# Softplus straight from PSUM on ScalarE, beside an attention that keeps Exp

## The chip, the cores and the metric

One core of a Trainium2 chip (trn2) runs the whole program. The metric is device time in microseconds (us) from start to end of one execution. TensorE (PE) multiplies matrices; PEld is its weight load, which overlaps the multiplication. VectorE (DVE) and ScalarE (ACT) do elementwise work, SyncE (SP) issues most transfers. Every engine runs its own list of instructions strictly in order and waits on counters of the others.

## The reference, cut to what matters

```python
# 4 batches, 8 heads, 576 positions, head size 64; window of 64 positions
attn = exp(scores - max); attn = attn / (sum(attn) + 1e-9)     # scores masked to 0 <= i-j < 64
x = attn @ v                                                    # -> 2304 tokens x 512
h = x @ w_in;  g = maximum(h, 0) + log1p(exp(-abs(h)))          # layer 0: 512 -> 2048, softplus
x = g @ w_out                                                   # 2048 -> 512
h = x @ w_in2; g = where(h >= 1, h, where(h <= -1, 0, (h + 1)**2 / 4))   # layer 1
out = g @ w_out2
```

All arrays are float32.

## The kernel before

**Tokens.** The 2304 tokens go in blocks: layer 0 takes 512, 256, 512, 512, 512 of them, called block 0 to block 4 here. Layer 1 takes the same tokens, the block of 256 last. 128 tokens are a double; there are 18 of them, 0 to 17.

**A step of a layer.** A step takes one group of 128 hidden columns (of 16, index f) for one block; in a block of 256 tokens it takes two groups at once, and for the first four groups of block 0 it takes half the block (the half steps). `g1` (L345) makes h in a PSUM bank from twelve products: weights and activations are each split into a high part (`wh`, `xh`) and a low part (`wl`, `xl`), and three of the four pairings are summed. The activation function then makes g, and `g2` (L357 in layer 0, L365 in layer 1) adds its products into four PSUM banks `y`. `g2` runs two steps late (`LAG = 2`), so between the end of a step's `g1` and the start of its `g2` four other groups of products stand on TensorE. h has two banks: the `g1` two steps later needs the last reader of h to be done.

**Softplus before.** ScalarE takes Abs of h (L383), Exp of the negative (L384), adds 1 (block 0: L386; else L388 on VectorE) and takes Ln (L389). VectorE corrects the rounding with L390 and L391 and adds max(h, 0) in L392, the last reader of h. Outside block 0, `parts` splits g into a high part `gh` (ScalarE, L373) and a low part `gl` (VectorE, L374); block 0 multiplies g undivided with undivided weights `wo`. Exp and Ln stand in one table of functions, which is loaded once, at L63.

**Attention.** The attention of a double is made while the block before it is multiplied: block 1's two doubles during block 0, block 2's four during block 1, and so on; block 0's own come first, the last two of them within the half steps. A double has four pieces, one to a step in blocks of 512: scores for half the heads (`sub_scores`, u = 0, which makes all score products, L220), scores for the other half (u = 1), transposes (L273) with masked evacuations (L286), and the products with v (L305) with the copies to `xh` (L312) and `xl` (L315). Inside `sub_scores`, `a1` copies from PSUM (ScalarE, L245 or L247), `d1` finds the maximum (VectorE, L251 to L253), `a2` takes four Exp with row sums (ScalarE, L257), and `d2` divides (VectorE, L261 to L263).

**Weights.** They arrive as packed words (`raw`, three buffers, SyncE, L116) and are decoded by one ScalarE instruction (L123) and three on VectorE (L124 to L126) in block 0. The input weights are split there (L133, L134); the `wo` are split for the later blocks by the end of block 0 and in block 1.

The code is written in program order, and a scheduler of the framework decides how the pieces interleave on each engine.

Of the kernel before, what the change touches and what calls it, by code (L numbers as in the profile page):

```python
# [8 lines left out]
F32 = mybir.dt.float32  # L9
F32R = mybir.dt.float32r  # L10
I32 = mybir.dt.int32
AF = mybir.ActivationFunctionType
ALU = mybir.AluOpType
# [4 lines left out]
P = 128  # L18
# [21 lines left out]
def tile_window_attention_two_ffn(  # L40
# [10 lines left out]
    V, A, T = nc.vector, nc.scalar, nc.tensor  # L51
# [5 lines left out]
    gpool = ctx.enter_context(tc.tile_pool(name="g", bufs=3))  # L57
    tpool = ctx.enter_context(tc.tile_pool(name="tmp", bufs=2))
# [1 line left out]
    psum = ctx.enter_context(tc.tile_pool(name="psum", bufs=1, space=bass.MemoryType.PSUM))  # L60
    dpool = ctx.enter_context(tc.tile_pool(name="dram", bufs=1, space=bass.MemoryType.DRAM))

    A.preload_act_table_set("natural_log_exp_and_others")  # L63


    ident = cpool.tile([P, P], F32, name="ident")
# [27 lines left out]
    def pt(tag):  # L94
        return psum.tile([P, 512], F32, tag=tag, name=tag, bufs={"y": 4, "h": 2, "a": 2}[tag])
# [130 lines left out]
    def sub_scores(dbl, u, bank):  # L226
        if u == 0:
            p2s[dbl] = apool.tile([P, NP, 2, CB], F32, tag="p2", name="p2")
        pr = p2s[dbl][:, 2 * u:2 * u + 2]
        sel = pr.rearrange("p a s j -> p (a s) j")  # L230
        mx = apool.tile([P, NP], F32, tag="mx", name="mx")
        sm = apool.tile([P, NP], F32, tag="sm", name="sm")

        def pe():
            if u == 0:
                scs[dbl] = score_products(dbl, bank)

        def a1():
            sc = scs[dbl][u]
            first = [s for s in range(2) if (2 * dbl + s) % NCB == 0]  # L240
            for s in first:
                V.memset(pr[:, :, s, :], MASKED)
            if first:
                s = 1 - first[0]
                A.copy(pr[:, :, s, :], sc[:, :, s, 0:CB])  # L245
            else:
                A.copy(pr, sc[:, :, :, 0:CB])  # L247

        def d1():
            sc = scs[dbl][u].rearrange("p a s j -> p (a s) j")  # L250
            V.copy_predicated(sel, msel.rearrange("p (o j) -> p o j", o=1).to_broadcast([P, NP, CB]), sc[:, :, CB:])  # L251
            V.tensor_reduce(mx, sel, axis=AX.X, op=ALU.max)
            sub_dve[dbl, u] = V.tensor_scalar_mul(mx, mx, -SCALE).ins  # L253

        def a2():
            for i in range(NP):
                A.activation(sel[:, i, :], sel[:, i, :], AF.Exp, bias=mx[:, i:i + 1], scale=SCALE,  # L257
                             accum_out=sm[:, i:i + 1])

        def d2():  # L260
            V.tensor_scalar_add(sm, sm, EPS)  # L261
            V.reciprocal(sm, sm)
            V.tensor_tensor(sel, sel, sm.rearrange("p (a o) -> p a o", o=1).to_broadcast([P, NP, CB]), op=ALU.mult)  # L263

        return pe, a1, d1, a2, d2

    def sub_transpose(dbl, bank):
        pr = p2s.pop(dbl)
        tp = pt(bank).rearrange("p (a c i) -> p a c i", a=NP, c=2)

        def pe():
            for a in range(NP):
                T.matmul(tp[:, a].rearrange("p c i -> p (c i)"), pr[:, a].rearrange("p c i -> p (c i)"), ident,  # L273
                         start=True, stop=True, is_transpose=True)

        pts[dbl] = [apool.tile([P, NP, 2, CB], F32, tag=f"pt{s}", name=f"pt{s}", bufs=1) for s in range(2)]
        o, n = slice(CB, P), slice(0, CB)

        def evac(s):
            t = pts[dbl][s]  # L280
            r = (n, o)[s]

            for m, dst in ((mown, o), (mprev, n)):
                if dst is n and (2 * dbl + s) % NCB == 0:
                    continue
                V.tensor_tensor(  # L286
                    t[dst].rearrange("p a c i -> p (a c) i"),
                    tp[r].rearrange("p a c i -> p (a c) i"),
                    m[r].rearrange("p (o i) -> p o i", o=1).to_broadcast([CB, 2 * NP, CB]),
                    op=ALU.mult)  # L290

        return pe, (lambda: None), (lambda: evac(0)), (lambda: None), (lambda: evac(1))
# [26 lines left out]
    def attn_subs(block, early=0):  # L319
        t0, n = block  # L320
        xh = xpool.tile([P, KC, 512], F32R, tag="xh", name="xh")
        xl = xpool.tile([P, KC, 512], F32R, tag="xl", name="xl")
        subs = []
        for i in range(n // P):
            dbl = t0 // P + i
            tag = "y" if i < early else "a"
            tag2 = "a" if i % 2 == 0 or i >= early else "h"
            subs += [
                (lambda dbl=dbl, tag=tag: sub_scores(dbl, 0, tag)),
                (lambda dbl=dbl, tag=tag: sub_scores(dbl, 1, tag)),  # L330
                (lambda dbl=dbl, tag=tag2: sub_transpose(dbl, tag)),
                (lambda dbl=dbl, tag=tag2, i=i: sub_pv(dbl, tag, xh, xl, i * P)),
            ]
        return subs, xh, xl
# [35 lines left out]
    def parts(e, n):  # L370
        gh = gpool.tile([P, 512], F32R, tag="gh", name="gh")[:, :n]
        gl = gpool.tile([P, 512], F32R, tag="gl", name="gl")[:, :n]
        A.copy(gh, e)  # L373
        V.tensor_tensor(gl, e, gh.bitcast(F32), op=ALU.subtract)  # L374
        return gh, gl

    def softplus(h, n, split):

        e = tpool.tile([P, 512], F32, tag="e", name="e")[:, :n]
        u = tpool.tile([P, 512], F32, tag="u", name="u", bufs=1)[:, :n]  # L380
        l = tpool.tile([P, 512], F32, tag="l", name="l", bufs=1)[:, :n]
        g = e if split else gpool.tile([P, 512], F32, tag="gl", name="g")[:, :n]
        A.activation(e, h, AF.Abs)  # L383
        A.activation(e, e, AF.Exp, scale=-1.0)  # L384
        if not split:
            A.activation(u, e, AF.Copy, bias=1.0)  # L386
        else:
            V.tensor_scalar_add(u, e, 1.0)  # L388
        A.activation(l, u, AF.Ln)  # L389
        V.scalar_tensor_tensor(e, u, 1.0, e, op0=ALU.subtract, op1=ALU.subtract)  # L390
        V.tensor_tensor(l, l, e, op=ALU.subtract)  # L391
        V.scalar_tensor_tensor(g, h, 0.0, l, op0=ALU.max, op1=ALU.add)  # L392
        return parts(g, n) if split else (g,)

    def quadratic(h, n, split):

# [40 lines left out]

    xs, ys = {}, {}
    subs, *xs[0, 0] = attn_subs(BLOCKS[0][0], HALF // P)
    nq = 4 * HALF // P  # L440
    for j in (0, 1, 4, 5, 2, 3, 6, 7)[:nq]:
# [34 lines left out]
    for layer, i, f, kf, c0, n in steps:  # L476
# [33 lines left out]
        h = pt("h")[:, :kf * n]  # L510
        for j in range(kf):
            g1(layer, f + j, c0, n, *xs[layer, i], h[:, j * n:(j + 1) * n])
        if len(pend) >= LAG:
            emit_g2(pend.pop(0))
        g = (softplus, quadratic)[layer](h, kf * n, (layer, i) != (0, 0))
        pend.append((layer, i, f, kf, c0, n, g))
    while pend:
# [38 lines left out]
```

## Time and profile before

| | |
|---|---|
| time, 3 runs | 908.78 us median, 906.93 to 909.26 |
| the profiled execution's own time | 910.36 us |
| its span, first to last instruction | 908.6 us |
| TensorE busy | 876.2 us (96%) |
| VectorE busy | 621.7 us (68%) |
| ScalarE busy | 425.8 us (47%) |

The profiled execution is 1.6 us above the median of the three runs, and 1.8 us of its time lie outside the span. Busy shares are averages over stages that differ: 0 to 32 us is the first attention, 32 to 75 us the half steps, 75 to 170 us the rest of block 0, 170 to about 230 us block 1, then blocks 2 to 4 up to 519 us, then layer 1.

### The profile page before, as it was taken

How to read it: one execution, taken by the hardware profiler on the slowest of the kernel's cores; microseconds unless marked ns; L12 is line 12 of the kernel's file. 1: busy time of each engine (PE TensorE's matmuls, PEld its weight loads, DVE VectorE, ACT ScalarE, POOL GpSimd, SP SyncE). 2: the span in 40 equal slices, each digit the busy share in tenths (PEclk: the TensorE clock that was granted, in tenths of full speed). 3: DMA queues.
4: the chain of work that ended last, by engine and by line, in shares of the span. 5: the costliest groups of instructions: out<-in, count | busy, mean ns of one | idle time of the engine just before them, and what ended most of it. 6: DMA issues, size and time to landing. Idle time of an engine off the chain costs nothing.

```text
span 908.6 us, 13022 instructions
## 1 busy us (share of the span) xinstructions
PE 876.2 (96%) x4984; PEld 713.6 (79%) x4984; DVE 621.7 (68%) x1166; ACT 425.8 (47%) x958; POOL 1.5 (0%) x10
## 2 busy tenths in 40 slices
PE   3889999899999999999999999999999999999998
PEld 2677656699888888888888888888888888888897
DVE  5899899797777787777999799854335333533342
ACT  5577684555455555554766455432223222322221
POOL 0000000000000000000000000000000000000000
PEclk9999999999999999999999999999999999999999
DMA  8474642334211231200632254120002000200010
GB/s 282 164 217 144 226 155 70 117 82 117 81 41 54 71 116 48 70 1 28 211 110 93 83 195 147 62 93 0 1 1 94 1 0 1 70 1 0 1 48 23
DMA packets 45374, 75.42 MB, mean 83 GB/s; under 512 B 4864, under 2 KB 21760, under 8 KB 45312
## 3 DMA queue, kind: packets, MB, share of 16 engines
q1 hardware_dynamic: 42912, 70.01, 23.9%
q10 hardware_dynamic: 2400, 4.59, 1.4%
q8 instruction: 39, 0.64, 0.3%
q14 instruction: 23, 0.19, 0.1%
HBM read 65.14 MB, written 9.44 MB: 82 GB/s over the span
## 4 chain that ended last, share of the span: by engine, by line
PE 83%; DVE 8%; DMA 3%; ACT 3%; issue 2%; SPq 0%; ACTq 0%; DVEq 0%
PE h L345 40%; PE y L365 22%; PE y L357 17%; DMA raw<-in_w 3%; PE a L305 2%; PE a L220 2%; DVE wl L134 1%; ACT p L257 1%; DVE pt L286 1%; PE a L273 1%; DVE l L391 1%; DVE e L390 1%; DVE wo L126 1%; DVE bits L125 1%; DVE g L392 1%
## 5 line engine op out<-in xcount | busy, mean ns | idle before, releaser
L345 PE MATMUL h<-xh,wh 128*128 128x512 f32 (+1 forms) x656 | 246.7, 376 | 4.5 <-DVE g L392 1.6
L345 PE MATMUL h<-xl,wh 128*128 128x512 f32 (+1 forms) x656 | 240.8, 367 | 0.5 <-DVE xl L315 0.3
L345 PE MATMUL h<-xh,wl 128*128 128x512 f32 (+1 forms) x656 | 240.6, 367 | 0.1
L345 PEld LDWEIGHTS h<-xh,wh 128*128 128x128 f32 x656 | 125.2, 191 | 30.0 <-ACT wh L133 3.7
L345 PEld LDWEIGHTS h<-xh,wl 128*128 128x128 f32 x656 | 125.3, 191 | 20.6 <-issue 0.3
L345 PEld LDWEIGHTS h<-xl,wh 128*128 128x128 f32 x656 | 125.2, 191 | 20.4 <-DVE xl L315 0.9
L373 ACT CAST gh<-e 128x512 fp32r<-128x512 f32 x128 | 79.4, 620 | 115.9 <-DVE e L392 68.5
L399 ACT ACTIVATE e<-e 128x512 f32<-128x512 f32 x72 | 45.5, 632 | 187.0 <-DVE e L398 186.9
L374 DVE TENSOR_TENSOR gl<-e,gh 128x512 fp32r<-128x512 f32 x128 | 88.3, 690 | 55.2 <-ACT gh L373 53.2
L398 DVE TENSOR_SCALAR e<-h 128x512 f32<-128x512 f32 x72 | 49.7, 690 | 104.1 <-PE h L345 104.1
L365 PE MATMUL y<-wh,gh 128*128 128x512 f32 x288 | 112.1, 389 | 0.0
L365 PE MATMUL y<-wl,gh 128*128 128x512 f32 x288 | 112.1, 389 | 0.0
L365 PE MATMUL y<-wh,gl 128*128 128x512 f32 x288 | 112.0, 389 | 0.0
L357 PE MATMUL y<-gh,wl 128*128 128x512 f32 (+1 forms) x256 | 93.2, 364 | 0.0
L357 PE MATMUL y<-gl,wh 128*128 128x512 f32 (+1 forms) x256 | 92.8, 362 | 0.0
L357 PE MATMUL y<-gh,wh 128*128 128x512 f32 (+1 forms) x256 | 92.8, 362 | 0.0
L400 DVE TENSOR_TENSOR e<-h,e 128x512 f32<-128x512 f32 x72 | 49.7, 690 | 41.0 <-ACT e L399 40.5
L365 PEld LDWEIGHTS y<-wh,gl 128*128 128x128 f32 x288 | 54.0, 188 | 11.3
L365 PEld LDWEIGHTS y<-wh,gh 128*128 128x128 f32 x288 | 54.1, 188 | 11.1
L365 PEld LDWEIGHTS y<-wl,gh 128*128 128x128 f32 x288 | 54.1, 188 | 10.8
L357 PE MATMUL y<-g,wo 128*128 128x512 f32 (+1 forms) x160 | 59.5, 514 | 0.0
L257 ACT ACTIVATE p<-p,mx 128x64 f32<-128x64 f32 x144 | 48.2, 336 | 23.7 <-DVE mx L253 23.6
(78 smaller groups left out, 1076.3 us busy)
## 6 DMA issues: line engine op xcount, KB each, us to landing
raw<-in_w SPq DMA_DIRECT2D x64, 512.0 KB, 3.9
qt<-in_q SPq DMA_DIRECT2D x34, 256.0 KB, 3.9
vt<-in_v SPq DMA_DIRECT2D x31, 256.0 KB, 2.9
kt<-in_k SPq DMA_DIRECT2D x29, 256.0 KB, 4.0
vt<-x2d SPq DMA_DIRECT2D x16, 256.0 KB, 5.4
x2d<-o SPq DMA_DIRECT2D x5, 512.0 KB, 2.9
out<-o SPq DMA_DIRECT2D x5, 512.0 KB, 3.1
x2d<-o ACTq DMA_DIRECT2D x4, 512.0 KB, 4.7
```

The lines of the kernel that those rows point to most:

```text
L125: V.scalar_tensor_tensor(t, hi, -2 ** 31, t, op0=ALU.bitwise_and, op1=ALU.bitwise_or)
L220: T.matmul(banks[u][o, a2, s, lo:], qt[r, a, r], kt[r, a, -(2 * CB - lo):], start=True, stop=True)
L257: A.activation(sel[:, i, :], sel[:, i, :], AF.Exp, bias=mx[:, i:i + 1], scale=SCALE, accum_out=sm[:, i:i + 1])
L305: T.matmul(po[hf * CB:(hf + 1) * CB, a, s, :], vts[s][r, hd:hd + D], pp[s][r, 2 * hf + a // 2, a % 2, :], start=True, stop=True)
L345: T.matmul(h, w, x, start=i == 0, stop=i == len(ops) - 1)
L357: T.matmul(y[m][:, c0:c0 + n], w, x, start=f + i + c0 == 0, stop=f == NF - 1 and i == len(ops) - 1)
L365: T.matmul(y[t], l, r, start=f == 0 and i == 0, stop=f == NF - 1 and i == 2)
L373: A.copy(gh, e)
L374: V.tensor_tensor(gl, e, gh.bitcast(F32), op=ALU.subtract)
L398: V.tensor_scalar(e, h, -1.0, 1.0, op0=ALU.max, op1=ALU.min)
L399: A.activation(e, e, AF.Square, bias=0.5, scale=0.5)
L400: V.tensor_tensor(e, h, e, op=ALU.max)
```

## The change

Softplus becomes a function that ScalarE applies to h itself. In block 0 one instruction writes g. Elsewhere ScalarE applies it twice, once with the output rounded to `gh` and once in full to `e`, and VectorE makes `gl` from the two; the five other instructions of VectorE and ScalarE are gone. Softplus and Exp are in different tables, so a table load stands wherever the two meet in ScalarE's list. For doubles 4 to 17 the two halves' maxima are found in one piece and all eight Exp stand in the next one.

```diff
-    A.preload_act_table_set("natural_log_exp_and_others")
+    A.preload_act_table_set("exp_and_others")
+    def sub_scores_gathered(dbl, u, bank, kept):
+        if u == 0:
+            kept[:] = [sub_scores(dbl, i, bank) for i in range(2)]
+            return [kept[0][0]] + [kept[i][j] for i in range(2) for j in (1, 2)]
+        return [kept[i][3] for i in range(2)] + [kept[i][4] for i in range(2)]
...
-                (lambda dbl=dbl, tag=tag: sub_scores(dbl, 0, tag)),
-                (lambda dbl=dbl, tag=tag: sub_scores(dbl, 1, tag)),
+            if t0 == 0:
+                subs += [(lambda dbl=dbl, tag=tag, u=u: sub_scores(dbl, u, tag)) for u in range(2)]
+            else:
+                subs += [(lambda dbl=dbl, tag=tag, u=u, kept=kept: sub_scores_gathered(dbl, u, tag, kept))
+                         for kept in [[]] for u in range(2)]
...
     def softplus(h, n, split):
-        A.activation(e, h, AF.Abs)
-        A.activation(e, e, AF.Exp, scale=-1.0)
-        if not split:
-            A.activation(u, e, AF.Copy, bias=1.0)
-        else:
-            V.tensor_scalar_add(u, e, 1.0)
-        A.activation(l, u, AF.Ln)
-        V.scalar_tensor_tensor(e, u, 1.0, e, op0=ALU.subtract, op1=ALU.subtract)
-        V.tensor_tensor(l, l, e, op=ALU.subtract)
-        V.scalar_tensor_tensor(g, h, 0.0, l, op0=ALU.max, op1=ALU.add)
-        return parts(g, n) if split else (g,)
+        if not split:
+            g = gpool.tile([P, 512], F32, tag="gl", name="g")[:, :n]
+            A.activation(g, h, AF.Softplus)
+            return (g,)
+        e = tpool.tile([P, 512], F32, tag="e", name="e")[:, :n]
+        gh = gpool.tile([P, 512], F32R, tag="gh", name="gh")[:, :n]
+        gl = gpool.tile([P, 512], F32R, tag="gl", name="gl")[:, :n]
+        A.activation(gh, h, AF.Softplus)
+        A.activation(e, h, AF.Softplus)
+        V.tensor_tensor(gl, e, gh.bitcast(F32), op=ALU.subtract)
+        return gh, gl
```

The built program has 53 table loads behind the first: one in front of the first softplus, two for double 3, four for double 4, six for double 5, two for each of doubles 6 to 9 and four for each of doubles 10 to 17. Three places show how the lists change.

**Place 1.** ScalarE in block 2, around the Exp of double 10 (`p_2376`). Before:

```order
L312 CAST xh<-a 128x4x128
L389 ACTIVATE l<-u 128x512
L373 CAST gh<-e 128x512
L247 COPY p_2376<-a 128x256 x2
L257 ACTIVATE p_2376,sm<-p_2376,mx 128x64 x4
L383 ACTIVATE e<-h 128x512
L257 ACTIVATE p_2376,sm<-p_2376,mx 128x64
L384 ACTIVATE e<-e 128x512
L257 ACTIVATE p_2376,sm<-p_2376,mx 128x64 x2
L389 ACTIVATE l<-u 128x512
L257 ACTIVATE p_2376,sm<-p_2376,mx 128x64
L373 CAST gh<-e 128x512
```

The same place now (`p_2132` is the same double):

```order
L319 CAST xh<-a 128x4x128
L247 COPY p_2132<-a 128x256 x2
L257 ACT_TABLE_LOAD
L257 ACTIVATE p_2132,sm<-p_2132,mx 128x64
L396 ACT_TABLE_LOAD
L396 ACTIVATE gh<-h 128x512
L397 ACTIVATE e<-h 128x512
L257 ACT_TABLE_LOAD
L257 ACTIVATE p_2132,sm<-p_2132,mx 128x64 x7
L396 ACT_TABLE_LOAD
L396 ACTIVATE gh<-h 128x512
```

One step's softplus stands between the first Exp and the other seven, so the double has four loads, three of them ahead of its last Exp; the load in front of the first Exp waits for the maximum, as that Exp did. On TensorE the four transposes still stand behind the double's score products and four groups of twelve products. The same rows return for doubles 11 to 17.

**Place 2.** VectorE at the end of block 0, ahead of the maxima of double 6 (`p_1485`). Before:

```order
L134 TENSOR_TENSOR wl_1969<-wo,wh_1968 128x512
L134 TENSOR_TENSOR wl_1973<-wo,wh_1972 128x512
L134 TENSOR_TENSOR wl_2074<-wo,wh_2073 128x512
L134 TENSOR_TENSOR wl_2078<-wo,wh_2077 128x512
L134 TENSOR_TENSOR wl_2200<-wo,wh_2199 128x512
L390 SCALAR_TENSOR_TENSOR e<-u,e 128x512
L134 TENSOR_TENSOR wl_2204<-wo,wh_2203 128x512
L391 TENSOR_TENSOR l<-l,e 128x512
L134 TENSOR_TENSOR wl_2304<-wo,wh_2303 128x512
L392 SCALAR_TENSOR_TENSOR g<-h,l 128x512
L251 COPY_PREDICATED p_1485<-msel,a 128x256 x2
L252 TENSOR_REDUCE mx<-p_1485 128x4 x2
```

The same place now (`p_1305` is the same double):

```order
L134 TENSOR_TENSOR wl_1757<-wo,wh_1756 128x512
L134 TENSOR_TENSOR wl_1761<-wo,wh_1760 128x512
L134 TENSOR_TENSOR wl_1854<-wo,wh_1853 128x512
L134 TENSOR_TENSOR wl_1858<-wo,wh_1857 128x512
L134 TENSOR_TENSOR wl_1972<-wo,wh_1971 128x512
L134 TENSOR_TENSOR wl_1976<-wo,wh_1975 128x512
L322 TENSOR_TENSOR xl<-a,xh 128x4x128
L134 TENSOR_TENSOR wl_2068<-wo,wh_2067 128x512
L251 COPY_PREDICATED p_1305<-msel,a 128x256 x2
L252 TENSOR_REDUCE mx<-p_1305 128x4 x2
L253 TENSOR_SCALAR mx<-mx 128x4 x2
```

The three softplus instructions are gone from the list, and all but two of the 16 splits of `wo` stand ahead of the last low part `xl` of block 1 (L322, L315 before), where seven and more stood behind it.

**Place 3.** TensorE in the half steps, between the transposes of double 2 and its products with v. Before:

```order
L273 MATMUL a<-ident,p_296 128x128 x2
L345 MATMUL h<-xl,wh_374 128x256
L345 MATMUL h<-xh,wl_375 128x256
L273 MATMUL a<-ident,p_296 128x128 x2
L305 MATMUL a<-pt_410,vt 64x64 x8
L345 MATMUL h<-xh,wh_450 128x256
L345 MATMUL h<-xl,wh_450 128x256
L357 MATMUL y<-g,wo 128x256 x3
L305 MATMUL a<-pt_411,vt 64x64 x8
L220 MATMUL a<-kt,qt 64x128 x8
```

Now, from the fourth row behind the last transpose:

```order
L355 MATMUL h<-xh,wl_442 128x256
L355 MATMUL h<-xh,wh_441 128x256
L355 MATMUL h<-xl,wh_441 128x256
L355 MATMUL h<-xh,wl_442 128x256
L355 MATMUL h<-xh,wh_441 128x256
L355 MATMUL h<-xl,wh_441 128x256
L355 MATMUL h<-xh,wl_442 128x256
L355 MATMUL h<-xh,wh_441 128x256
L355 MATMUL h<-xl,wh_441 128x256
L355 MATMUL h<-xh,wl_442 128x256
L312 MATMUL a<-pt_401,vt 64x64 x8
L367 MATMUL y<-g,wo 128x256 x2
```

The products with v, which stood right behind the transposes, now stand behind the whole `g1` of the third half step.

## Rows read from the trace of the kernel before

**Rows 1.** The page: busy time of each engine, share of the span, instructions.

```profile
PE 876.2 (96%) x4984; PEld 713.6 (79%) x4984; DVE 621.7 (68%) x1166; ACT 425.8 (47%) x958; POOL 1.5 (0%) x10
```

**Rows 2.** Windows by stage: length, busy time by engine, granted clock, DMA share, GB/s.

```profile
32.00:75.00 43.00, 36.80 (x285) 31.23 (x285) 38.36 (x99) 30.53 (x101) 0.00 (x0) 0.96 0.63 205
...
75.00:170.00 95.00, 90.14 (x462) 58.77 (x461) 87.44 (x165) 61.76 (x132) 0.00 (x0) 0.98 0.39 130
...
170.00:230.00 60.00, 59.45 (x599) 53.66 (x596) 48.20 (x108) 34.23 (x110) 0.00 (x0) 1.00 0.40 117
...
230.00:414.00 184.00, 184.00 (x1230) 149.47 (x1229) 141.89 (x278) 98.16 (x256) 0.00 (x0) 1.00 0.19 60
...
519.00:908.00 389.00, 385.40 (x1790) 322.68 (x1789) 194.29 (x303) 121.03 (x199) 0.00 (x0) 1.00 0.14 46
```

**Rows 3.** Waits of TensorE, whole run: total us, times, longest.

```profile
PE a L273 <- DVE p L263: 5.3, 5, 2.6
...
PE a L305 <- DVE pt L286: 4.2, 4, 1.8
...
PE h L345 <- DVE g L392: 1.6, 2, 0.9
```

**Rows 4.** Timeline of TensorE: start, length, engine, instruction, [idle before <-releaser].

```profile
40.16 0.69 PE L305 MATMUL a<-pt,vt 128*64 128x64 f32 x16 [1.83 <-DVE pt L286]
...
119.00 0.47 PE L345 MATMUL h<-xh,wh 128*128 128x512 f32 x1 [1.32 <-DVE sm L262]
...
161.99 0.41 PE L273 MATMUL a<-ident,p 128*128 128x128 f32 x2 [2.58 <-DVE p L263]
...
163.31 0.41 PE L273 MATMUL a<-ident,p 128*128 128x128 f32 x2 [0.92 <-DVE p L263]
```

**Rows 5.** Timeline of VectorE and ScalarE, end of block 0.

```profile
151.45 3.59 DVE L134 TENSOR_TENSOR wl<-wo,wh 128x512 fp32r<-128x512 f32 x5
...
157.96 0.76 DVE L251 COPY_PREDICATED p<-msel,a 128x256 f32<-128x256 int32 x2
...
159.53 0.35 ACT L257 ACTIVATE p<-p,mx 128x64 f32<-128x64 f32 x1 [5.93 <-DVE mx L253]
```

**Rows 6.** Windows right behind that wait, columns as in rows 2.

```profile
163.40:164.40 1.00, 1.00 (x10) 1.00 (x11) 0.90 (x2) 0.51 (x2) 0.00 (x0) 1.00 0.00 0
...
164.40:168.00 3.60, 3.60 (x30) 3.32 (x28) 3.49 (x7) 0.78 (x2) 0.00 (x0) 0.53 0.00 0
```

**Rows 7.** Groups by line and shape: busy us, mean ns | idle before.

```profile
L384 ACT ACTIVATE e<-e 128x512 f32<-128x512 f32 x68 | 42.8, 630 | 1.5
...
L373 ACT CAST gh<-e 128x512 fp32r<-128x512 f32 x128 | 79.4, 620 | 115.9 <-DVE e L392 68.5 <-DVE e L400 47.1
...
L383 ACT ACTIVATE e<-h 128x512 f32<-128x512 f32 x68 | 40.2, 591 | 21.6 <-PE h L345 21.3 <-ACT wh L133 0.3
...
L390 DVE SCALAR_TENSOR_TENSOR e<-u,e 128x512 f32<-128x512 f32 x68 | 47.0, 690 | 2.4 <-ACT u L386 0.8
...
L63 ACT ACT_TABLE_LOAD x1 | 1.3, 1283 | 0.8 <-PEq L546 0.8
```

**Rows 8.** Timeline of one double's attention in block 2, all engines.

```profile
269.41 1.10 PE L220 MATMUL a<-kt,qt 64*64 64x128 f32 x32
...
271.33 0.64 ACT L247 COPY p<-a 128x256 f32<-128x256 f32 x2
...
273.72 0.35 ACT L257 ACTIVATE p<-p,mx 128x64 f32<-128x64 f32 x1 [1.75 <-DVE mx L253]
...
274.06 0.33 ACT L257 ACTIVATE p<-p,mx 128x64 f32<-128x64 f32 x1
...
275.60 0.43 DVE L263 TENSOR_TENSOR p<-p,sm 128x256 f32<-128x256 f32 x1
...
279.31 0.43 DVE L263 TENSOR_TENSOR p<-p,sm 128x256 f32<-128x256 f32 x1
...
281.50 0.60 PE L273 MATMUL a<-ident,p 128*128 128x128 f32 x4
```

More of the change, by code (lines that the diff above doesn't have):

```diff
@@ L377, in softplus @@
     def softplus(h, n, split):
+        if not split:
+            g = gpool.tile([P, 512], F32, tag="gl", name="g")[:, :n]
+            A.activation(g, h, AF.Softplus)
+            return (g,)
         e = tpool.tile([P, 512], F32, tag="e", name="e")[:, :n]
-        u = tpool.tile([P, 512], F32, tag="u", name="u", bufs=1)[:, :n]
-        l = tpool.tile([P, 512], F32, tag="l", name="l", bufs=1)[:, :n]
-        g = e if split else gpool.tile([P, 512], F32, tag="gl", name="g")[:, :n]
-        A.activation(e, h, AF.Abs)
-        A.activation(e, e, AF.Exp, scale=-1.0)
-        if not split:
-            A.activation(u, e, AF.Copy, bias=1.0)
-        else:
-            V.tensor_scalar_add(u, e, 1.0)
-        A.activation(l, u, AF.Ln)
-        V.scalar_tensor_tensor(e, u, 1.0, e, op0=ALU.subtract, op1=ALU.subtract)
-        V.tensor_tensor(l, l, e, op=ALU.subtract)
-        V.scalar_tensor_tensor(g, h, 0.0, l, op0=ALU.max, op1=ALU.add)
-        return parts(g, n) if split else (g,)
+        gh = gpool.tile([P, 512], F32R, tag="gh", name="gh")[:, :n]
[4 more added lines that the diff above has]
+        return gh, gl
     def quadratic(h, n, split):
```

## The prediction

> **What bounds the kernel now.** The page's first part comes first: TensorE is busy for 876.2 of 908.6 us, the two engines that the change relieves are at 68 and 47% [rows 1]. So the change cannot gain what it takes off VectorE or ScalarE. It can gain only time in which TensorE stands still. The windows by stage say where that is [rows 2]: in blocks 2 to 4 (230 to 414 us) TensorE is busy for 184.00 of 184 us, and in layer 1 it stands only at the end, 3.6 us of 389, where no softplus is near. Between 32 and 230 us it stands for 6.2 us in the half steps, 4.9 us in the rest of block 0 and 0.55 us in block 1, together 11.6 us. There VectorE is busy for 38.4 of 43 and 87.4 of 95 us, and ScalarE for less. The waits of TensorE and the timeline name the partner, VectorE [rows 3, 4].
>
> The largest wait can be followed whole. At 161.99 us the transposes of double 6 start 2.58 us late, the second pair 0.92 us more [rows 4]. The maxima stood in VectorE's queue behind splits of `wo`, five of them in one row, and behind the three softplus instructions (place 2): ScalarE had been done with the copies that they read since 153.60 us (159.53 less its 5.93 us idle), VectorE took the next step, L251, only at 157.96 us [rows 5]. And the wait costs more than itself. The granted clock is 1.00 (2.4 GHz) up to 164.4 us and 0.53 (nearly all at 1.2 GHz) from there to 168.0 us [rows 6], though TensorE is busy throughout, so at full clock about 3.6 x (1 - 0.53) = 1.7 us of that stretch would not be there.
>
> **What leaves and what comes, by engine.** Of the softplus VectorE loses 76 x 3 instructions of at most 0.69 us and 56 shorter ones, at most 196 us at the price of L390; ScalarE loses 76 Exp, 20 additions, 76 Ln and 56 casts, 228 instructions of at most 0.63 us (144 us), and gains 56 second passes (33 us at 0.59 us, the price of L383, which reads the same tile from PSUM) and 53 table loads (68 us at the one load's 1.283 us) [rows 7]. Both engines end up with less work, so neither becomes the bound by its sum. A softplus itself gets shorter: four passes of ScalarE and five of VectorE in a row become two and one, which is why nothing in `g2` or in the h banks should wait. What can be late is what stands behind a load, and that is the attention.
>
> **The gains, step by step.** (a) 75 to 170 us, 4.9 us of waiting: 1.32 us at 119.00 us and the 3.5 us of double 6 [rows 4]. For double 6, VectorE's order now has the splits earlier and the three instructions are gone; with L251 at 153.6 instead of 157.96 us and one load of 1.28 us in front of the Exp, the probabilities are ready 3.1 us earlier, at 158.9 where the transposes were wanted at 161.99 - 2.58 = 159.4 us. The second pair was ready at 163.31 us, now at 160.2 us; eight products of 256 columns stand ahead of it, and it just fits. I take 4.8 us. The bounds are 0, if VectorE is still behind, and 4.9. (b) The half clock behind that wait, 1.7 us; 0 if a wait of the same size stays. (c) Half steps, 6.2 us. The longest wait, 1.83 us at 40.16 us [rows 4], was for evacuations that now have a whole `g1` in front of the products with v (place 3); the h-bank waits of 1.6 us in all on L392 [rows 3] go, since the bank's last reader is now ScalarE's own pass. But seven loads fall into or just behind this stretch, and the decoding of weights binds as well, so I take half, 3.1 us, between 0 and 6.2. Together 9.6 us.
>
> **The losses.** Blocks 2 and 3 have no slack to gain in and eight doubles (10 to 17) with three loads ahead of the last Exp (place 1). I count from the end of the score products, 269.41 + 1.10 = 270.51 us in the double shown [rows 8]. ScalarE is free there now, so the copy L247 can start at 0 instead of 0.8; from its start to the first Exp 2.39 us passed. So: load from 2.4 to 3.7, one Exp of 0.35, load to 5.3, two softplus passes of 0.59 to 6.5, load to 7.8, then Exp every 0.34 us. The fourth Exp of the first half ends at 8.8. From that end to the divided probabilities 0.95 us passed in the trace (273.72 + 3 x 0.34 + 0.35 = 275.09, to 275.60 + 0.43), so the first half is ready at 9.8 and the second at 7.8 + 7 x 0.34 + 0.95 = 11.1. The transposes start at 281.50 - 270.51 = 11.0, the second pair a little later. Before, the second half was ready at 279.74 us, 1.8 us ahead. So that reserve is spent and the second pair stands on the edge: every 0.1 us by which a load holds ScalarE longer than its row costs 0.3 us in each of the eight doubles.
>
> How much longer, no row shows: the one load stands at the start, with nothing behind it for microseconds. The lower bound is nothing. The upper is one instruction of ScalarE, 0.63 us, that would have to drain first [rows 7]. I take 0.1 us, nearer the bottom, as the row is a whole instruction's time and its neighbours in the trace follow each other within a tenth. That makes 0.3 us, with 0.1 for the edge 0.4 us a double, 3.2 us for eight. Doubles 6 to 9 have one load ahead of their Exp; 6 fits (above), for 7 to 9 I take 0.5 us in all, between 0 and 3 x 1.28 us. Softplus behind the Exp comes later too, but two further groups of products stand in front of the `g1` that needs its bank; I take nothing for that. Sum of the losses: 3.7 us.
>
> **A page against this change.** The Trainium skill says, in "ScalarE: Activation LUTs", section "What ACT_TABLE_LOAD costs", that a switch is a load of about 1283 ns and a drain of about 1380 ns; its "Rules for kernel authors" want all of one set done before switching. The trace agrees with the first number (1283 ns) and shows nothing of a drain. By that page's total the loss would be 28 x 1.28 us more than mine (the 28 is derived below), and the time about 939 us. "ScalarE activation tables: per-element evaluation and per-set limits", section "What a function is on this engine", gives one load of 1283 ns and no drain, by which my sum stands.
>
> **The sum.** 9.6 - 3.7 = 5.9 us less. The profiled execution took 910.36 us and would take 904.5; the median of before is 1.6 us lower, so 908.78 - 5.9 = 903 us.
>
> **Rivals.** *A load holds ScalarE longer (slower).* In doubles 10 to 17 three loads count, in 6 to 9 one: 8 x 3 + 4 = 28 loads on TensorE's path. With 0.63 us beyond the row instead of 0.1 the loss grows by 28 x 0.53 = 14.8 us: 918 us. It decides from 0.1 + 5.9 / 28 = 0.31 us on, a load of 1.6 us in place. Against it speaks only the row of the load; for it, that nothing behind that load was in a hurry. Waits of over 2 us could also bring the half clock, as in rows 6.
>
> *The weights bind block 0.* In the half steps the DMA engines are busy for 0.63 of the time and moved 205 GB/s [rows 2]; if raw words arrive no earlier, TensorE waits for weights instead of for VectorE, and (c) and the 1.3 us of (a) stay. Then 3.5 + 1.7 - 3.7 = 1.5 us less: 907.3 us. Against it: none of the larger waits of TensorE is on the weights.
>
> *All of it goes and nothing new comes.* 11.6 + 1.7 = 13.3 us less, 895.5 us. Place 1 speaks against it.
>
> **How the numbers follow.** My forecast has 0.54, the longer load 0.20, the weights 0.18, the full gain 0.08. The forecast's own range is 898 to 906 us. A measurement of this kernel tells about 0.3% (2.7 us) from no change: forecast, but for its top edge, and full gain are faster, 0.59; the weights' case and that edge are the same, 0.20; the longer load is slower, 0.21. The range 895 to 919 us reaches to the full gain and to the longer load at its bound, and leaves out a load far above that bound.
>
> **What would show it.** Right: windows of 75 to 170 us with TensorE standing for under 1 us and a clock of 1.00 where the old stretch was; table loads of 1.28 us whose neighbours follow within 0.1 us; transposes in blocks 2 and 3 with waits of under 0.5 us each on the division (L263). Wrong: waits of 1 us or more there, in each of eight doubles; or waits of TensorE in the half steps on `wh` or `wl`. If VectorE is no longer near full between 75 and 160 us and TensorE still waits there, step (a) has failed.

## The result and the profile after

The changed kernel takes 900.94 us (median of four runs, 900.64 to 901.92) where the kernel before takes 909.02 us (906.93 to 910.48): a ratio of 0.9915, 95% interval 0.9894 to 0.9936, or 8.1 us less. Forecast were 903 us and a range of 895 to 919 us. The profiled execution took 901.92 us, with a span of 900.2 us; 8.4 us less than the profiled one of before. Executions of one kernel differ by up to 7 us, along with the mean granted clock that they got (the kernel before, run beside e5: 905.24 us at 0.999, 912.30 us at 0.992), so a difference of a few us between single executions may be chance.

Line numbers have moved: `g1` is now L355, `g2` of layer 0 L367, the transposes L280, their evacuations L293, the products with v L312, `xh` and `xl` L319 and L322; softplus is L391 in block 0 and L396 to L398 elsewhere. In the experiments' kernels they can stand a few numbers later; e9 has the numbers of before. The page's first part, to be held against [rows 1]:

```profile
PE 875.6 (97%) x4984; PEld 713.8 (79%) x4984; DVE 468.5 (52%) x882; ACT 397.0 (44%) x839; POOL 1.5 (0%) x10
```

VectorE lost 153 us of work and ScalarE 29 us, and neither is what the kernel gained. The windows by stage (columns as in [rows 2]) say more:

```profile
32.00:75.00 43.00, 39.99 (x289) 34.11 (x289) 30.14 (x72) 29.42 (x76) 0.00 (x0) 0.88 0.59 196
75.00:170.00 95.00, 93.59 (x516) 60.49 (x515) 71.23 (x135) 54.30 (x110) 0.00 (x0) 1.00 0.44 143
170.00:230.00 60.00, 60.00 (x591) 55.56 (x592) 30.44 (x74) 37.70 (x103) 0.00 (x0) 1.00 0.36 104
230.00:414.00 184.00, 184.00 (x1215) 149.22 (x1210) 67.14 (x152) 98.49 (x224) 0.00 (x0) 1.00 0.18 57
```

In the half steps TensorE stands for 3.0 us instead of 6.2, but its granted clock fell from 0.96 to 0.88. From 75 to 170 us it stands for 1.4 us instead of 4.9; in blocks 2 to 4 for nothing, as before.

Where the time came from is seen best between fixed pieces of work: from TensorE's first `g1` to the first of block 1 (stretch A: half steps and the rest of block 0), to the first of block 2 (stretch B, block 1), to layer 1's first `g2` (stretch C, blocks 2 to 4), to TensorE's end (stretch D). The starts are read from TensorE's timeline, in us:

| | first g1 | A | B | C | D | TensorE's end |
|---|---|---|---|---|---|---|
| before | 31.53 | 121.30 | 67.62 | 298.83 | 385.13 | 904.41 |
| after | 30.68 | 121.04 | 60.50 | 298.61 | 385.13 | 895.96 |

The first `g1` starts between 29.88 and 31.56 us in all the programs of this study, so the 0.85 us ahead of it are taken as chance. **Nearly the whole gain, 7.1 us, lies in stretch B.** By windows over A and B, TensorE was busy for 113.74 and 63.58 us before and is for 116.53 and 60.44 us now. So in A 3.05 us of standing went and 2.8 us of busy time came (the half clock there cost 1.7 us before, by granted clocks of 0.89, 0.50 and 0.76 in the windows of 2 us from 40 to 46 us, and costs 5.1 us now); in B both fell, standing by 3.98 us (4.04 to 0.06) and busy time by 3.1 us. Of these 3.1 us 1.7 are the half clock ([rows 6]: 3.6 us at 0.53; B's clock is 1.00 now); 1.1 us come from the score products of double 8, which stood in two pieces of 16, 1.09 us each, and now stand in one of 32 that takes 1.10 us. The second piece of before, and the piece now:

```profile
189.57 1.09 PE L220 MATMUL a<-kt,qt 64*64 64x128 f32 x16
...
181.71 1.10 PE L220 MATMUL a<-kt,qt 64*64 64x128 f32 x32
```

TensorE's timeline where waits were, and where new ones are (columns as in [rows 4]):

```profile
49.93 0.41 PE L280 MATMUL a<-ident,p 128*128 128x128 f32 x2 [0.57 <-DVE p L263]
51.25 0.41 PE L280 MATMUL a<-ident,p 128*128 128x128 f32 x2 [0.91 <-DVE p L263]
53.19 0.70 PE L367 MATMUL y<-g,wo 128*128 128x256 f32 x2 [1.53 <-ACT g L391]
...
123.20 0.50 PE L355 MATMUL h<-xh,wh 128*128 128x512 f32 x1 [1.12 <-ACT wh L133]
...
124.17 0.51 PE L355 MATMUL h<-xh,wl 128*128 128x512 f32 x1 [0.23 <-DVE wl L134]
...
158.13 0.38 PE L280 MATMUL a<-ident,p 128*128 128x128 f32 x2
...
159.51 0.41 PE L280 MATMUL a<-ident,p 128*128 128x128 f32 x2
```

The last two rows are double 6's transposes, which waited for 2.58 and 0.92 us before and now for nothing. The first three are double 3, in the half steps: its eight Exp stand behind a table load, and the next softplus behind another, so three waits lie within 4 us. What follows them is in the windows of two microseconds (the three left out between the first and the second row have 0.50 each):

```profile
54.00:56.00 2.00, 2.00 (x25) 1.24 (x24) 1.96 (x5) 0.67 (x1) 0.00 (x0) 0.58 0.25 32
...
62.00:64.00 2.00, 2.00 (x12) 1.78 (x13) 0.35 (x2) 0.27 (x1) 0.00 (x0) 0.50 0.16 64
64.00:66.00 2.00, 2.00 (x25) 1.93 (x22) 0.70 (x2) 1.09 (x4) 0.00 (x0) 0.86 0.00 0
66.00:68.00 2.00, 2.00 (x18) 1.97 (x18) 1.97 (x6) 1.97 (x4) 0.00 (x0) 1.00 0.89 277
```

From 54 to about 64.5 us TensorE is busy throughout, for some 10 us at 1.2 GHz (a granted clock of 0.50); by these windows it costs about 5 us.

The wait at 123.20 us is new too. The weights had arrived, and VectorE had ended their decoding (L126) at 112.19 us. The timelines of VectorE and ScalarE show why they were late: their cast stood behind double 5's Exp and five loads among them (the first and the last are shown).

```profile
111.50 0.69 DVE L126 SCALAR_TENSOR_TENSOR bits<-raw,bits 128x512 int32<-128x512 int32 x1
...
111.95 1.28 ACT L257 ACT_TABLE_LOAD   x1 [0.40 <-DVE mx L253]
...
120.58 1.28 ACT L257 ACT_TABLE_LOAD   x1
...
122.55 0.60 ACT L133 CAST wh<-bits 128x512 fp32r<-128x512 f32 x1
```

Block 2, place 1 of the change, from the score products of double 10 to its transposes, on all engines:

```profile
261.16 1.10 PE L220 MATMUL a<-kt,qt 64*64 64x128 f32 x32
...
262.32 0.65 ACT L247 COPY p<-a 128x256 f32<-128x256 f32 x2 [2.68 <-PE a L220]
...
264.28 1.28 ACT L257 ACT_TABLE_LOAD   x1 [1.32 <-DVE mx L253]
...
265.58 0.35 ACT L257 ACTIVATE p<-p,mx 128x64 f32<-128x64 f32 x1
...
266.02 1.28 ACT L396 ACT_TABLE_LOAD   x1
...
267.32 0.60 ACT L396 ACTIVATE gh<-h 128x512 fp32r<-128x512 f32 x1
...
267.81 0.59 ACT L397 ACTIVATE e<-h 128x512 f32<-128x512 f32 x1
...
268.42 1.28 ACT L257 ACT_TABLE_LOAD   x1
...
272.60 0.42 DVE L263 TENSOR_TENSOR p<-p,sm 128x256 f32<-128x256 f32 x1
...
273.26 0.60 PE L280 MATMUL a<-ident,p 128*128 128x128 f32 x4
```

Every load takes 1.28 us; what stands behind it starts 0.02 us after its end, and it starts 0.02 us after the end of what stands ahead. The division ends at 273.02 us, 0.24 us ahead of the transposes. They do not wait, here or in any of doubles 10 to 17.

### The profile page after: what moved, and what is told of

Same layout as the page of the kernel before. It is cut to its first block, busy times and chain, and to the rows that moved or that the text cites. A ratio compares the mean times of both kernels' runs of the same rounds, so it can differ in the third digit from the quotient of the medians.

```text
span 900.2 us, 12527 instructions
## 1 busy us (share of the span) xinstructions
PE 875.6 (97%) x4984; PEld 713.8 (79%) x4984; DVE 468.5 (52%) x882; ACT 397.0 (44%) x839; POOL 1.5 (0%) x10
## 4 chain that ended last, share of the span: by engine, by line
PE 90%; DVE 3%; DMA 3%; ACT 2%; issue 0%; SPq 0%; ACTq 0%; DVEq 0%
PE h L355 43%; PE y L375 22%; PE y L367 21%; DMA raw<-in_w 3%; PE a L220 2%; PE a L312 2%; PE a L280 1%; DVE pt L293 1%; ACT p L257 1%; ACT L257 0%; ACT L391 0%; DVE wl L134 0%; ACT bits L123 0%; DVE bits L125 0%; DVE bits L126 0%
## 5 line engine op out<-in xcount | busy, mean ns | idle before, releaser
L355 PE MATMUL h<-xh,wh 128*128 128x512 f32 (+1 forms) x656 | 246.9, 376 | 1.8 <-ACT wh L133 1.1
L355 PE MATMUL h<-xh,wl 128*128 128x512 f32 (+1 forms) x656 | 241.5, 368 | 0.2 <-DVE wl L134 0.2
L355 PE MATMUL h<-xl,wh 128*128 128x512 f32 (+1 forms) x656 | 241.5, 368 | 0.1
L355 PEld LDWEIGHTS h<-xh,wh 128*128 128x128 f32 x656 | 125.4, 191 | 26.0 <-issue 2.3
L355 PEld LDWEIGHTS h<-xh,wl 128*128 128x128 f32 x656 | 125.5, 191 | 21.2 <-DVE wl L134 1.3
L355 PEld LDWEIGHTS h<-xl,wh 128*128 128x128 f32 x656 | 125.5, 191 | 20.2 <-issue 0.7
L367 PE MATMUL y<-gh,wh 128*128 128x512 f32 (+1 forms) x256 | 93.2, 364 | 0.0
L367 PE MATMUL y<-gl,wh 128*128 128x512 f32 (+1 forms) x256 | 93.0, 363 | 0.0
L367 PE MATMUL y<-gh,wl 128*128 128x512 f32 (+1 forms) x256 | 92.9, 363 | 0.0
L398 DVE TENSOR_TENSOR gl<-e,gh 128x512 fp32r<-128x512 f32 x56 | 38.5, 688 | 88.4 <-ACT e L397 88.3
L383 ACT CAST gh<-e 128x512 fp32r<-128x512 f32 x72 | 44.7, 621 | 47.2 <-DVE e L406 47.1
L396 ACT ACTIVATE gh<-h 128x512 fp32r<-128x512 f32 x56 | 33.4, 597 | 69.7 <-PE h L355 69.5
L367 PE MATMUL y<-g,wo 128*128 128x512 f32 (+1 forms) x160 | 61.8, 522 | 1.5 <-ACT g L391 1.5
```

The lines of the kernel that those rows point to most:

```text
L355: T.matmul(h, w, x, start=i == 0, stop=i == len(ops) - 1)
L367: T.matmul(y[m][:, c0:c0 + n], w, x, start=f + i + c0 == 0, stop=f == NF - 1 and i == len(ops) - 1)
L396: A.activation(gh, h, AF.Softplus)
```

## The experiments

Each was run beside the kernel before on one chip, so its ratio is its own. A to C are the stretches above, from the profiled execution alone.

| run | time, us | ratio [95%] | A | B | C |
|---|---|---|---|---|---|
| e1_block0_only | 901.72 | 0.9913 [0.9887, 0.9939] | 119.30 | 62.43 | 298.69 |
| e2_blocks14_only | 905.67 | 0.9947 [0.9933, 0.9961] | 120.52 | 64.61 | 298.60 |
| e3_vector_back | 899.42 | 0.9894 [0.9876, 0.9912] | 117.46 | 61.23 | 298.62 |
| e4_scalar_back | 902.88 | 0.9915 [0.9889, 0.9941] | 122.18 | 60.69 | 298.62 |
| e5_no_gather | 900.28 | 0.9900 [0.9882, 0.9918] | 119.38 | 60.48 | 298.60 |
| e6_extra_switch | 902.59 | 0.9921 [0.9898, 0.9943] | 121.85 | 60.49 | 301.13 |
| e7_half_steps_old | 900.36 | 0.9890 [0.9877, 0.9904] | 119.62 | 60.51 | 298.61 |
| e8_early_load | 894.81 | 0.9832 [0.9819, 0.9844] | 114.68 | 60.43 | 298.59 |
| e9_splits_behind | 905.95 | 0.9956 [0.9942, 0.9971] | 121.82 | 62.73 | 298.58 |
| e10_hold_one | 897.75 | 0.9876 [0.9859, 0.9892] | 117.25 | 60.47 | 298.59 |
| e11_hold_two | 899.56 | 0.9898 [0.9881, 0.9916] | 118.61 | 60.46 | 298.60 |

Letters of theories are those of each quoted expectation.

### Which part of the change gives the gain: e1, e2

The new softplus in block 0 alone, and in blocks 1 to 4 alone; the other blocks keep the old one. Both keep the gathering of the Exp by doubles.

```diff
 # e1, in softplus
+        if split:
...
+            return softplus_old(h, n, split)
 # e2, in softplus
+        if not split:
+            return softplus_old(h, n, split)
```

In e1 the table with Exp and Ln is loaded again behind the last softplus of block 0.

> The new softplus in block 0 alone; blocks 1 to 4 have the old one, with one switch back to the table of Exp and Ln behind block 0 and no switch after it. Theory A (the gain comes from VectorE's queue at the end of block 0, so that double 6's transposes are on time): the transposes of double 6 wait under 1 us, no half clock behind them, 901 to 905 us. Rival B (the gain comes from block 1's own shorter softplus, since the stretch from the first product of block 1 to the first of block 2 went from 67.6 to 60.5 us): that stretch stays above 65 us, 906 to 909 us.

> The new softplus in blocks 1 to 4 alone, the old one in block 0; 40 loads; the splits of wo and block 0's three softplus instructions stand ahead of double 6's maxima as in the kernel before. If all of the gain comes from block 0: double 6 waits as before, 3 to 5 us (one load more in front of its Exp), the half clock behind it stays, and the time is 907 to 912 us, no faster than before. If the new softplus of blocks 1 to 4 is worth something by itself: the stretch of block 1 falls below 65 us and the time below 905 us.

Block 0 alone gives as much as the whole change (0.9913 against 0.9915). So the theory of block 0 holds (double 6 waits for nothing there, and B is 62.43 us, where its rival wanted over 65); but e2 fell between its two cases. Blocks 1 to 4 alone give 4.0 us, though the whole change is only 0.8 us ahead of e1 (900.94 and 901.72 us). The two parts overlap: in e2 double 6 still waits, for 2.61 us instead of 3.50, and the half clock behind it costs 1.7 us, as before. TensorE's timeline and windows in e2:

```profile
160.20 0.41 PE L280 MATMUL a<-ident,p 128*128 128x128 f32 x2 [1.69 <-DVE p L263]
161.52 0.41 PE L280 MATMUL a<-ident,p 128*128 128x128 f32 x2 [0.92 <-DVE p L263]
```

```profile
160.00:165.00 5.00, 3.88 (x22) 3.71 (x23) 4.13 (x10) 2.87 (x7) 0.00 (x0) 0.74 0.00 0
165.00:170.00 5.00, 5.00 (x46) 3.17 (x46) 2.63 (x4) 2.03 (x4) 0.00 (x0) 0.92 0.25 72
```

Besides, double 8's score products stand in one piece there, which is 1.1 us. With the 0.9 us less of waiting and double 9's wait of 0.45 us, which is gone, that makes 2.4 of the 3.0 us by which B fell; the rest is not traced.

### What made double 6 late, work or order: e3, e4, e9

e3 gives VectorE three passes back for each softplus of block 0, e4 gives ScalarE three copies. Their results are used by nobody.

```diff
 # e3
             A.activation(g, h, AF.Softplus)
...
+            V.scalar_tensor_tensor(l, g, 1.0, g, op0=ALU.subtract, op1=ALU.subtract)
+            V.tensor_tensor(l, l, g, op=ALU.subtract)
+            V.scalar_tensor_tensor(l, g, 0.0, l, op0=ALU.max, op1=ALU.add)
 # e4
             A.activation(g, h, AF.Softplus)
...
+            A.activation(l, g, AF.Copy)
+            A.activation(l, l, AF.Copy)
+            A.activation(l, l, AF.Copy)
```

> The changed kernel, and VectorE makes three further passes of the old kind (0.69 us for 512 columns) behind each softplus of block 0, on a tile that nobody reads; ScalarE as in the changed kernel. Theory A (VectorE's queue): double 6's transposes wait 2 us or more again, with the half clock behind them, 905 to 909 us. Rival C (the gain comes from ScalarE's shorter passes and the earlier release of h): 900 to 902 us, no such wait.

> The changed kernel, and ScalarE makes three further copies (0.6 us each for 512 columns) behind each softplus of block 0, on a tile that nobody reads, so that ScalarE has its old four passes there; VectorE as in the changed kernel. Theory A (VectorE's queue): 900 to 903 us, at most a few tenths of further waits. Rival C (ScalarE's shorter passes): 906 to 909 us.

Both keep the gain. In e4 ScalarE is busy for 75.64 of the 95 us from 75 to 170, where the changed kernel has 54.30, and B stays at 60.7 us: its shorter list is not the cause. In e3 VectorE is as full as before (87.01 of 95 us, before 87.44, [rows 2]), and double 6 still waits for only 0.79 us. So theory A, which gave 2 us or more, fell in that form: with VectorE's work back, the long wait does not return. But the edit also changed the order, so it does not show that less work is worth nothing. What differs from the kernel before is what stands ahead of the maxima. VectorE's timeline in e3, and TensorE's wait:

```profile
149.37 0.77 DVE L251 COPY_PREDICATED p<-msel,a 128x256 f32<-128x256 int32 x2
...
151.47 2.87 DVE L134 TENSOR_TENSOR wl<-wo,wh 128x512 fp32r<-128x512 f32 x4
...
155.76 0.41 PE L280 MATMUL a<-ident,p 128*128 128x128 f32 x2 [0.79 <-DVE sm L262]
```

The maxima (L251) start at 149.37 us, and the last splits of `wo` (L134) stand behind them; in [rows 5] the splits stood ahead.

In the changed kernel, though, the splits do stand ahead (place 2), and so they do in e4. VectorE there, first in the changed kernel, then in e4:

```profile
141.10 8.81 DVE L134 TENSOR_TENSOR wl<-wo,wh 128x512 fp32r<-128x512 f32 x12
...
152.24 0.78 DVE L251 COPY_PREDICATED p<-msel,a 128x256 f32<-128x256 int32 x2 [1.00 <-ACT p L247]
```

```profile
148.59 4.38 DVE L134 TENSOR_TENSOR wl<-wo,wh 128x512 fp32r<-128x512 f32 x6
152.89 0.78 DVE L251 COPY_PREDICATED p<-msel,a 128x256 f32<-128x256 int32 x2
```

In the changed kernel VectorE had been idle for 1.00 us when the copy that the maxima read was done; in e4 six splits stand right ahead of them, and TensorE still stands for only 0.18 us in B. With the three softplus instructions gone the queue is through in time although the splits keep their place; with them there and the splits ahead (e2, whose other blocks have the new softplus) double 6 waits for 2.61 us.

e9 tests the order alone: it is the kernel before with its old softplus everywhere and one edit, which holds ten of the sixteen splits (ScalarE's casts and VectorE's subtractions) until double 6's maxima are in the list.

```diff
             while osplit[0] < min(f + kf, NF):
-                halves((0, osplit[0]), wo.pop(osplit[0]), 1)
+                with tc.issue_after(sub_dve[6, 1]) if osplit[0] >= 6 else ExitStack():
+                    halves((0, osplit[0]), wo.pop(osplit[0]), 1)
```

> The kernel before with its own softplus everywhere; only the splits of wo from the seventh on are held until double 6's maxima are in VectorE's list. VectorE does the same work, and the three softplus instructions still stand ahead of the maxima. Theory A (order: the wait of double 6 comes from the splits that stand ahead of its maxima): the two waits at 162 us (2.58 and 0.92 us) fall below 0.5 us together, the half clock behind them goes, and the stretch from the first g1 of block 1 to that of block 2 falls from 67.6 to 61 to 62 us; time 902 to 904.5 us, 5 to 7 below before. Theory B (it takes the shorter softplus, not the order): double 6 still waits for 2 us or more and the time is 907 to 910 us.

VectorE and TensorE in e9, and the windows behind:

```profile
152.49 0.78 DVE L251 COPY_PREDICATED p<-msel,a 128x256 f32<-128x256 int32 x2 [0.72 <-ACT p L247]
...
158.38 0.38 PE L273 MATMUL a<-ident,p 128*128 128x128 f32 x2
...
159.11 0.41 PE L273 MATMUL a<-ident,p 128*128 128x128 f32 x2
```

```profile
160.00:165.00 5.00, 5.00 (x39) 3.28 (x38) 4.86 (x8) 2.14 (x4) 0.00 (x0) 1.00 0.04 7
165.00:170.00 5.00, 5.00 (x64) 3.66 (x64) 4.84 (x9) 2.52 (x6) 0.00 (x0) 1.00 0.69 238
```

The maxima now wait for their copy, not in VectorE's queue; both waits of the transposes are gone, and the clock stays at 1.00. B falls by 4.9 us to 62.73 us. The time is 905.95 us, 3.8 below before and under half of the changed kernel's 8.1; theory A gave 5 to 7, so it missed there. Still, **order alone, with nothing of softplus touched, removes the wait and its half clock**; the 2.2 us that B is still above the changed kernel's are 0.4 us of smaller waits, double 8's score products in two pieces (1.1 us), and a rest that is not traced. So what made double 6 late is VectorE's queue ahead of its maxima, and either cure is enough: fewer instructions with the splits in their place (the changed kernel, e4), or the splits behind with all the instructions there (e9).

### What loads cost in blocks 2 and 3: e5, e6

e5 leaves out the gathering by doubles; e6 puts two more loads into each of doubles 10 to 17, with a softplus of a single column between the fourth and the fifth Exp, so that five stand ahead of the last Exp.

```diff
 # e5
-            if t0 == 0:
+            if True:
                 subs += [(lambda ...: sub_scores(dbl, u, tag)) for u in range(2)]
 # e6, in sub_scores_gathered, for doubles 10 to 17
-        return [kept[i][3] for i in range(2)] + [kept[i][4] for i in range(2)]
+        return [kept[0][3], (lambda: A.activation(s1[:, 0:1], s0[:, NP - 1:NP], AF.Softplus)), kept[1][3],
+                kept[0][4], kept[1][4]]
```

> The changed kernel without the gathering by doubles: each half's Exp stands in its own piece, in ScalarE's list four Exp, load, two softplus, load, four Exp in doubles 10 to 17; 54 loads as well, and still three ahead of a double's last Exp. Theory A (the gain lies in block 0 and block 1, TensorE waits for nothing in blocks 2 to 4): the stretch from block 2's first g1 to layer 1's first g2 stays at 298 to 299 us, time 899 to 903 us, no different from the changed kernel. Rival G (the gathering is what kept the doubles of blocks 2 and 3 in time): 0.4 us or more in each of eight doubles, stretch of 302 us or more, time 904 us or more.

> The changed kernel with a softplus of one column between the fourth and the fifth Exp of doubles 10 to 17, which adds two table loads to each: 70 loads instead of 54. If the transposes of these doubles are on the edge (the reserve in the trace is about 0.2 us): their second pair comes about 2.5 us late in each of the eight doubles, 20 us, and up to 1.7 us of half clock each on top: 919 to 935 us. If they have a larger reserve than I read: under 905 us. The loads should have 1.28 us each and their neighbours follow within 0.1 us.

Without the gathering nothing changes (0.9900, C 298.60 us): it has as many loads ahead of a double's last Exp. e6 costs 2.5 us in C, 0.3 us for each of the eight doubles, not the 20 us that an edge would have cost. Its list shows why: the scheduler moved the transposes. They stand in two pieces between later products, and TensorE is busy for 183.96 of the 184 us from 230 to 414, at full clock. So the 2.5 us are products that take longer in the new order, not waits.

```profile
272.11 1.28 ACT L275 ACT_TABLE_LOAD   x1
...
273.63 1.28 ACT L257 ACT_TABLE_LOAD   x1
...
274.64 0.40 PE L284 MATMUL a<-ident,p 128*128 128x128 f32 x2
...
277.19 0.38 PE L284 MATMUL a<-ident,p 128*128 128x128 f32 x2
```

### What the half steps lose: e7, e8, e10, e11

e7 keeps the old softplus in the first four half steps. e8 adds one Exp of a single column behind double 3's first score copy, so that the load of the table runs while VectorE looks for the maxima. e10 and e11 are e8 with the decoding of one or two half steps' weights (`split_w`) held behind double 3's division.

```diff
 # e8, at the end of a1 in sub_scores
+            if u == 0 and dbl == 3:
+                tiny = apool.tile([P, 1], F32, tag="tiny", name="tiny")
+                A.activation(tiny, pr[:, 0, 0, 0:1], AF.Exp, scale=0.0)
 # e10 (e11: wsplit[0] in (3, 4)); sub_div holds the divisions of d2
-                with tc.issue_after(sub_dve[0, 1]) if wsplit[0] == 0 else ExitStack():
+                hold = sub_dve[0, 1] if wsplit[0] == 0 else sub_div.get((3, 1)) if wsplit[0] in (4,) else None
+                with tc.issue_after(hold) if hold is not None else ExitStack():
                     split_w(*divmod(wsplit[0], NF))
```

> The changed kernel with the old softplus in the first four half steps, so that double 3's Exp needs no load there (48 loads). Theory D (the load in front of double 3's Exp and the one in front of the next softplus cause the waits at 50 to 53 us and the half clock behind them): the granted clock between 32 and 75 us goes back from 0.88 to about 0.96, and the stretch from the first g1 to the first step of 512 tokens falls by 1 to 4 us from 41.8 us; time 897 to 900 us. Rival E (the half steps wait for something else, the weights or the order): stretch 41 to 43 us and time 900 to 902 us.

> The changed kernel with one Exp of a single column right behind the first score copy of double 3, so that the load of the Exp table runs while VectorE still looks for the maxima; 54 loads, nothing else edited. Theory D: double 3's Exp start 1 to 1.4 us earlier, the two waits of the transposes at 50 and 51 us (1.5 us in all) fall below 0.5 us, the half clock behind them shortens, and the stretch from the first g1 to the first step of 512 tokens falls by 2 to 5 us from 41.8 us; time 896 to 899 us. Rival E: the wait only moves to the products with g (1.5 us or more) and the time is 900 to 902 us.

> The kernel with the early load of the Exp table, and the decoding of one half step's weights held until double 3's division is in VectorE's list, so that two decoding instructions (1.1 us) no longer stand between the division's three and ScalarE has one decoding less ahead of the next softplus. Theory D (what waits at 50 us is double 3's chain through ScalarE and VectorE): the wait of 2.38 us falls to 1 to 1.5 us, the half clock behind it (0.54 to 0.61 over 4 us) shortens or goes, time 891 to 894 us. Rival E (the weights bind there): the held decoding comes back as a wait of 1 us or more on the weights or on g, time 894 to 897 us.

> As the run before, with the weights of two half steps held behind double 3's division; the scheduler then puts a whole g1 behind double 3's transposes, so that TensorE has work while the evacuations and the next softplus run. Theory D: no wait on g is left in the half steps, the waits there sum to 1 to 2 us, time 890 to 894 us. Rival E: TensorE waits for wh or wl by 1 us or more between 55 and 75 us, time 895 to 899 us.

e8 is the fastest kernel of the study: 894.81 us, its interval below that of the changed kernel. Its half steps take 37.8 us up to the first step of 512 tokens (69.18 less 31.38 us), 4.0 less, as theory D had it; but not in D's way, as its timeline and its windows show:

```profile
43.79 1.28 ACT L250 ACT_TABLE_LOAD   x1
...
47.17 0.35 ACT L260 ACTIVATE p<-p,mx 128x64 f32<-128x64 f32 x1 [0.59 <-DVE mx L256]
...
52.42 0.41 PE L283 MATMUL a<-ident,p 128*128 128x128 f32 x2 [2.38 <-DVE p L266]
53.23 2.92 PE L370 MATMUL y<-g,wo 128*128 128x256 f32 x8 [0.40 <-ACT g L394]
```

```profile
54.00:56.00 2.00, 2.00 (x6) 1.18 (x4) 1.93 (x4) 0.87 (x3) 0.00 (x0) 0.54 0.32 129
56.00:58.00 2.00, 2.00 (x37) 1.85 (x38) 1.72 (x4) 0.73 (x2) 0.00 (x0) 0.61 0.03 8
58.00:60.00 2.00, 1.83 (x24) 1.56 (x22) 1.45 (x3) 1.21 (x3) 0.00 (x0) 1.00 0.80 213
```

The load is off the path: the first Exp waits for its maximum, no longer for the table. But the waits there still sum to 2.8 us, against 3.0 before the edit. What went is the clock behind them: it is back at 1.00 by 58 us instead of 66. Over A, TensorE is busy for 111.58 us instead of 116.53 and stands for 3.10 instead of 4.51, of which 1.35 us is the wait on the weights at 123 us, which e8 does not have. So of the 6.4 us in A some 3.4 are clock (5.1 us lost against 1.7, by the windows), 1.4 are standing and the rest shorter busy time that is not traced. The clock is not all of it: of the executions of the changed kernel one had a mean clock of 0.997 and took 901.01 us, and two of e8 with 0.997 took 894.81 and 894.96 us. That the early load itself brought the gain is not shown, since the edit changed the order of TensorE's products there too; and e3, whose load stands in front of double 3's Exp as in the changed kernel, has half steps of 37.6 us as well (68.10 less 30.46 us), with about 3.4 us of half clock behind a wait of 3.35 us.

e7 has no load at double 3, a clock of 0.92 from 32 to 75 us, but waits nearly as before (37.57 of 43 us busy), and its half steps take 42.9 us (73.21 less 30.32 us): that is rival E's case. But VectorE has its old softplus work again in these half steps, so e7 does not tell what the load alone costs. e10 shortens the wait to 1.47 us, then 0.87 us for g, as D had it; the clock gains nothing more on e8 (0.96 from 32 to 75 us in both), and the wait on the weights behind double 5's loads is back (1.12 us at 119.11 us); its time, 897.75 us, is above what either theory gave. e11 waits for its weights for 2.62 us at 54.22 us, as its rival had it, a little earlier than the 55 us that it named; its 899.56 us are just above that rival's range.

## Why the prediction was right, step by step

The sign, the place of the main gain and the size were right (5.9 us forecast, 8.1 measured). Two terms of the sum were wrong by about 4 us each, one up and one down, and cancelled; that the sum came so near is partly luck.

- **(a) 4.8 us, of which double 6 3.5 us:** right for double 6, which no longer waits. The cause was put in two parts, the splits' order and the three instructions; e4 shows that it is enough that the instructions are gone, and e9 that the order is enough. The other 1.3 us, at 119 us, were not gained: a wait of 1.12 and 0.23 us on weights stands in their place, behind double 5's loads. Six loads were counted for that double under the change, but the prediction priced none of them, neither on the way to its probabilities nor for the cast queued behind them.
- **(b) 1.7 us of half clock:** right; B's granted clock is 1.00 now, and 1.7 us was the cost by the windows of before.
- **(c) 3.1 us in the half steps:** the step that failed. The waits fell about as taken, by 3.2 us from 32 to 75 us. But no clock was counted there, and the waits that are left, three within 4 us, are followed by some 10 us at half clock, about 5 us where 1.7 were lost before. A as a whole gave 0.26 us where 4.4 (3.1 and the 1.3 above) were forecast. e8 has nearly as much waiting in the half steps and 6.4 us less time in A.
- **The losses, 3.7 us:** mis-sized; they are nothing. The chain of double 10 was worked out well: 11.0 us from the end of the score products to the transposes were forecast and 273.26 - 262.26 = 11.0 measured, the second half ready at 11.1 against 10.76 us. The 0.1 us for a load beyond its row is 0.02 us at each end, and the edge held by 0.24 us. Nor did two further loads bring the waits of an edge: in e6 the scheduler put the transposes later.
- **Not in the sum:** 1.1 us of double 8's score products and 0.45 us of double 9's wait in B.
- **The rivals.** The longer load fell: 53 loads of 1283 ns, with neighbours at 0.02 us. The weights do bind once, at 123 us, but because of ScalarE's list and not of the transfers. (A wait of 0.91 us on `wh` stands in the half steps of the kernel before too, at 51.42 us; the prediction passed over it.) The full gain was not reached: the clock in the half steps stood against it, and 4.5 us of standing that is left in A.
- **The signs.** The clock of 1.00, the loads' neighbours and the transposes without waits in blocks 2 and 3 came as named. TensorE standing for under 1 us from 75 to 170 us did not: it stands for 1.4 us, nearly all of it the wait on weights.

The Trainium skill's "ScalarE: Activation LUTs", section "What ACT_TABLE_LOAD costs", has a drain of about 1380 ns beside the load; the rows of block 2 above have the load and no drain. The Trainium skill's "ScalarE activation tables: per-element evaluation and per-set limits", section "What a function is on this engine", has the load alone, and the trace agrees (1283 ns).

What stays open: why the half clock lasts some 10 us behind three waits of 3.0 us in sum and about 3.4 us behind two of 2.8 us in e8. The work behind them differs in order as well, and no run here parts the two. Nor is the clock fixed by the kernel: e1 took 899.69 us at a mean clock of 0.997 and 904.88 us at 0.992.

## What to carry to other kernels

Before crediting a leaner function with a stall that it may remove, try the order of the list alone: one line that held ten splits back removed the same wait, though it gave under half of the whole gain. Price what a wait that you leave costs behind it in clock, not only its own length. A table load on the path can be moved into idle time by an instruction of one column that needs the same table; e8 shows the move, not what it is worth.

## What the runs showed of the hardware that was not expected

- A load of the function table takes 1283 ns in each of the 54 here and of the 70 in e6, whatever stands ahead of it, and delays its neighbours by 0.02 us beyond that.
- The score products of a double take 1.10 us as one piece of 32 and 1.09 us for each half when 16 stand alone between other products.
